# Scores on 64-row halves of the array, another order of zero writes, weight splits and gathers in a retention, mixture-of-experts and MLP kernel

## The chip, the cores and the metric

The kernel runs on one core of a Trainium2 chip. The metric is the device time of one execution in microseconds (us), the median over several runs. The core has a matrix engine (PE, with its weight loads shown as PEld), two elementwise engines (DVE and POOL), an activation engine (ACT), and SP, which here only issues transfers. POOL issues the indirect transfers (gathers). Sixteen DMA engines move the data.

## What is computed

```python
scores = scale * q @ k^T                                  # 4 batches, 8 heads, 576 tokens, 64 per head
Dmat = where(rel >= 0, gamma ** rel, 0)                   # rel = query position - key position
x = (scores * Dmat) @ v                                   # retention, -> 2304 tokens x 512
noisy = x @ w_gate + log1p(exp(x @ w_noise)) * noise      # 8 experts
top2, weights = two largest per token, softmax over them
for each expert e:                                        # 2304 x 512 -> 1024 -> 512
    out[its tokens] += weight * relu(x @ w1[e]) @ w2[e]
h = out @ w_in                                            # 512 -> 2048
result = (h * cos(h)) @ w_out                             # 2048 -> 512
```

## The kernel before, in words

Three stages follow one another on the matrix engine, and each prepares the next. Every float32 product is written as one instruction in the code and shows as two passes in the trace, so 8 products of a tile are 16 PE instructions.

**Tiles.** Retention runs over 20 tiles of 128 tokens, five per batch, the fifth with 64 rows from each of two halves ("tail"). One step `j` of the loop `for j in range(-2, NTILE + 1)` has the work of several tiles in it: `load_tile(j + 4)` issues the loads of Q (`qr`, L329), K (`kb`, L335) and K, V row-wise (`kv`, L343) on SP's queue, in order behind the stores of finished rows (`xs<-xr`, four per tile, L514) and, at the end of some steps, a 1 MB write of zeros into the unused part of the experts' output (`zero_overflow`, L373, `ys<-c_zero`). `decay(j + 2)` multiplies Q by its decay factors (L419 `qt<-qr`, on POOL from tile 4 on). `scores(j + 1)` makes K·Q for two heads at a time: a head has 64 dimensions, and two heads lie one above the other in the 128 rows. K is kept in a tile with zeros, rows 0 to 63 in one copy and rows 64 to 127 in another, so that each of the 8 products runs over all 128 rows (L445) and the zeros drop the other head. DVE multiplies each half of the result by the mask (L446, `am`). `outputs(j)` (L469, L474, L488) makes the attention rows; L474 has 64 result columns per product, in the left or right half of the array. `gate` and `gate_t` (L501, L521) start the choice of experts.

**Routing.** After the last tile of a group (6, 6, 4 and 4 tiles) a generator `routing(g)` counts where each token stands in its expert's list. It needs DVE for many small operations (`sa`, `sb`, L646 and L647, among them) and PE for counting ("rank", L606 to L615) and for tables (L638, `ptab<-sb,sa`). Its steps are let in by a planner: `spent(pe, dve)` adds the planned time of what was just written out, and `pump()` writes routing steps as long as the planned DVE queue is less than a slack ahead of PE. So the numbers given to `spent` decide how early routing stands on the engines.

**First expert.** The first layer of expert 0 for its first 320 tokens (`layer1(0, 0, True)`, L797) needs only the first groups; it starts at 123.96 us. It and its second layer (`layer2(0, 0, True)`, L818) are the loop `for k, _ in enumerate(post)`, with the rest of the routing pumped in between. In it stand the splits of expert 0's second weights `b0` to `b3` into a high and a low part (`split_unit`: ACT copies `hb`, L289; the engine named subtracts, `lb`, L290; then the next weight load is issued) at the steps `B_AT`, and more zero writes, at the steps `ZERO[i] - 20`. When the last group's table is there, `gidx` (L668) has the token numbers, POOL gathers three blocks of rows (L727, `rows<-xs,gidx`), PE turns them (L764), ACT and DVE split them, and `layer1(0, 1)` follows (L797, first at 167.00 us).

**Last layer.** After the eight experts, nine blocks of 256 tokens go through `fetch` (16 gathers on POOL, L1152, `y<-ys,slot`), `turn2` (weighted sum, turn, split into `x2h` and `x2l`), `mlp1` (PE L1192; then per part `g`, DVE and ACT make `t`, `gh`, and DVE or POOL makes `gl`, L1210) and `mlp2` (L1222). `fetch(0)` reads only the rows that are written early; `fetch(1)` and later read all rows of `ys`, so they stand behind the last expert's stores (L831, L835). Block 0 also has the splits of the last weights in it, `b0` to `b3` and `d0` to `d3`. `FS0` is the number of gathers of block 1 issued per step of `mlp1` in block 0, `SP0` the steps that have a split, `SPP` those on POOL, `GLP0` how many `gl` of block 0 go to POOL.

Of the kernel before, what the change touches and what calls it, by code (L numbers as in the profile page):

```python
# [10 lines left out]
F32 = mybir.dt.float32  # L11
# [6 lines left out]
OP = mybir.AluOpType  # L18
# [6 lines left out]
HP = H // 2  # L25
NC = 5
# [16 lines left out]
PHB = 3  # L43
STB = 3
QPOOL = 4
ZERO = (11, 13, 22, 27, 27, 29, 33)
LOOK = 4
WJ = 3
T0_AT = ()
GLP = 8  # L50
GLP0 = 4
FS = 1
FS0 = 1
SPP = (0, 3, 6, 9)
SP0 = (0, 1, 2, 3, 4, 5, 6, 7, 8, 9)

CG_1 = (6, 8, 9, 11, 13, 15)
CG_2 = (1, 2, 3, 4, 5)
# [18 lines left out]
B_US = 1.1  # L77
# [4 lines left out]
PE_LAT = 0.2  # L82
SPLIT_POOL = False
L1_WAIT = 2
B_AT = (0, 1, 2, 24)
B_POOL = range(99)
TURN_AT0 = (1, 1, 2, 3, 4)
GN = max(z - a for a, z in GRP)
EARLY_N = GRP[EARLY - 1][1] // NC * S + GRP[EARLY - 1][1] % NC * 128
# [125 lines left out]
def moe_kernel(ctx, tc, x, out, dbg=None, phases="ABC"):  # L215
    nc = tc.nc
# [14 lines left out]
    ps = ctx.enter_context(tc.tile_pool(name="ps", bufs=1, space=PSUM))  # L231
# [65 lines left out]
    ca = A.enter_context(tc.tile_pool(name="ca", bufs=1))  # L297
# [13 lines left out]
    bs = {n: cb[:, a:b] for n, (a, b) in OB.items()}  # L311
    dq0 = ca.tile([128, HP * 128 + (NC - 1) * HP], F32, name="dq0")
    dq = [dq0[:, :HP * 128]] + [ca.tile([128, HP * 128], F32, name=f"dq{c}") for c in range(1, NC)]
    KB = []
    for i in range(LOOK):
        t = ca.tile([128, HP, 2, 128], F32, name=f"kb{i}")
        eng = nc.gpsimd if i else nc.vector
        eng.memset(t[:64, :, 1, :], 0.0)
        eng.memset(t[64:, :, 0, :], 0.0)
        KB.append(t)  # L320
    KBT = ca.tile([128, HP, 2, TAIL], F32, name="kbt")
    SB = [ca.tile([128, HP, 128], F32, name=f"sb{i}") for i in range(2)]
# [2 lines left out]
    KT, KV, QR, QT, VT, AM, XT, XR, G = {}, {}, {}, {}, {}, {}, {}, {}, {}  # L325
# [4 lines left out]

    def load_k(j):
        b, c = divmod(j, NC)
        kb, src = (KB[(4 * b + c) % LOOK], x["kt"][4 * b + c]) if c < 4 else (KBT, x["ktt"][b])
        for s in range(2):
            nc.sync.dma_start(kb[s * 64:(s + 1) * 64, :, s, :],  # L335
                              src[s * 64:(s + 1) * 64].rearrange("p (a t) -> p a t", a=HP))
        KT[j] = kb

    def load_kv(j):
        b, c = divmod(j, NC)  # L340
# [44 lines left out]
    for i in range(2):  # L385
        t = rt.tile([128, GN, 2 * E], F32, name=f"lg{i}")
# [49 lines left out]
    def scores(j):  # L436
        b, c = divmod(j, NC)
        am = wk.tile([128, HP, 2, 128], F32, name="am", bufs=2)
        if c < 4:
            for h2 in range(2):  # L440
                p = ps.tile([128, 2, 2, 128], F32, name="ph", bufs=PHB)
                for i in range(2):
                    hp = 2 * h2 + i
                    for s in range(2):
                        nc.tensor.matmul(p[:, i, s, :], KT[j][:, hp, s, :], QT[j][:, hp, :], start=True, stop=True)  # L445
                nc.vector.tensor_tensor(  # L446
                    am[:, 2 * h2:2 * h2 + 2].rearrange("p a s q -> p (a s) q"),
                    p.rearrange("p a s q -> p (a s) q"),
                    bs["mask"][:, None, :].to_broadcast([128, 4, 128]), op=OP.mult)
                AM[j] = am  # L450
                yield
        else:
            p = ps.tile([128, HP, 128], F32, name="ph", bufs=PHB)
            for hp in range(HP):
                nc.tensor.matmul(p[:, hp, :], KT[j][:, hp].rearrange("p s q -> p (s q)"), QT[j][:, hp, :],
                                 start=True, stop=True)
            nc.vector.tensor_tensor(am[:, :, 0, :], p, bs["maskt"][:, None, :].to_broadcast([128, HP, 128]),
                                    op=OP.mult)
            AM[j] = am
            yield  # L460
# [383 lines left out]
    def spent(pe, dve=0.0):  # L844

        at["P"] += pe
        if dve:
            at["D"] = max(at["D"], at["P"] + PE_LAT) + dve
# [48 lines left out]
    for j in range(-2, NTILE + 1):  # L897
        if j >= 0:
            load_tile(j + LOOK)
        if j == WJ - 2:  # L900
            for _ in range(3):
                load_unit()
        if 0 <= j + 2 < NTILE:
            decay(j + 2)
        if j == -2:
            late = late_consts()
            next(late)
        pump()
        tail = j % NC == NC - 1
        if 0 <= j + 1 < NTILE:  # L910
            decay_v(j + 1)
            for _ in scores(j + 1):
                spent(0.87, 0.6)
                pump()
        if j >= -1:
            next(late, None)
        turn_early()
        if 0 <= j - 1 < NTILE:
            gate(j - 1)
            spent(0.37, 0.6)  # L920
        pump()
        fill(LF[0])
        if 0 <= j < NTILE:
            outputs(j)
            spent(1.75 if tail else 2.8)
        fill(LF[1])
        pump()
        turn_early()
        if 0 <= j - 1 < NTILE:
            gate_t(j - 1)  # L930
            spent(0.11, 0.13)
            for gi, (_, z) in enumerate(GRP):
                if z == j:
                    gens.append([routing(gi), 0])
        fill(LF[2])
        if j < NTILE:
            pump()
        for i in range(7):
            if ZERO[i] == j:
                zero_overflow(i)  # L940
        if j >= WJ and state["split"] < 4:
            split_unit(nc.gpsimd if SPLIT_POOL else nc.vector)
            if not SPLIT_POOL:
                spent(0, 1.1)
# [7 lines left out]
    for k, _ in enumerate(post):  # L952
        spent(0.33, L_US)
        pump()
        if k in T0_AT and not gens:
            turn(0, late[0])
            late[0] += 1
        if k in B_AT:
            split_unit(nc.gpsimd if k in B_POOL else nc.vector)
            if k not in B_POOL:  # L960
                spent(0, B_US)
        for i in range(7):
            if ZERO[i] == NTILE + k:
                zero_overflow(i)
# [211 lines left out]
    def mlp1(i, parts):  # L1176

        cw = state["d"]
        P, T = {}, {}

        def fl(t):
            return t.rearrange("p a b -> p (a b)")

        for s in range(10):
            if s < 8:
                w = W[8 * E + s]
                p = bank_h([128, 2, 256])
                for f in range(2):
                    k = 0
                    for a, b in PASSES:  # L1190
                        for dc in range(DC):
                            nc.tensor.matmul(p[:, f, :], w[a][:, dc, f * 128:(f + 1) * 128], X2[i][b][:, dc, :],  # L1192
                                             start=(k == 0), stop=(k == 3 * DC - 1))
                            k += 1
                P[s] = fl(p)
                t = T[s] = cw.tile([128, 512], F32, name="t", bufs=4)
                nc.scalar.activation(t, P[s], AF.Identity, scale=INV2PI, bias=cbias[:, 0:1])  # L1197
                nc.vector.tensor_scalar(t, t, -MAGIC, None, op0=OP.add)  # L1198
                nc.vector.scalar_tensor_tensor(t, t, -2 * PI, P[s], op0=OP.mult, op1=OP.add)
                nc.vector.tensor_scalar(t.bitcast(I32), t.bitcast(I32), 0x7FFFFFFF, None, op0=OP.bitwise_and)  # L1200
            if 0 <= s - 1 < 8:
                t = T[s - 1]
                nc.scalar.activation(t, t, AF.Sin, scale=-1.0, bias=cbias[:, 1:2])  # L1203
                nc.vector.tensor_tensor(t, t, P[s - 1], op=OP.mult)
            if 0 <= s - 2 < 8:
                g = s - 2
                gh = cw.tile([128, 2, 256], F32R, name=f"gh{g}")
                gl = cw.tile([128, 2, 256], F32R, name=f"gl{g}")
                nc.scalar.activation(fl(gh), T[g], AF.Copy)
                (nc.gpsimd if g < (GLP if i else GLP0) else nc.vector).tensor_tensor(  # L1210
                    fl(gl), T[g], fl(gh.bitcast(F32)), op=OP.subtract)
                parts.append((gh, gl))
            yield
# [21 lines left out]
    def drain(g):  # L1235
        for _ in g:
            pass

    def steps(g, n):
        for _ in range(n):  # L1240
            next(g, None)
# [12 lines left out]
    for e in range(E):  # L1254
# [3 lines left out]
        n = 0  # L1258
# [43 lines left out]
    for i in range(len(blocks)):  # L1302
        parts = []
        n = 0
        fg = fetch(i + 1)
        for _ in mlp1(i, parts):
            if n in SP0 and state["split"] < len(units):
                split_unit(nc.gpsimd if n in SPP else nc.vector)
            steps(fg, FS if i else FS0)
            n += 1  # L1310
        while state["split"] < len(units):
            split_unit()
        drain(fg)
        drain(turn2(i + 1))
        if i + 1 < len(blocks):
            mlp2(i, (0, 1), parts)
        else:
            mlp2(i, (0,), parts)
            mlp2(i, (1,), parts, ((0, DM // 2), (DM // 2, DM)))
# [18 lines left out]
```

## Time and profile before

| | |
|---|---|
| timed, 3 runs | 1069.2 us median (1066.33 to 1070.52) |
| the profiled execution, its own time | 1059.2 us |
| its span in the trace | 1057.3 us |
| PE busy | 995.3 us (94%) |
| PEld / DVE / POOL / ACT busy | 928.5 / 688.6 / 445.8 / 370.1 us |
| mean granted clock of PE | 0.966 |

The span runs from the first to the last instruction; the time of an execution has 1.9 us more around it. The timed runs lie above the profiled one by 7 to 11 us. A busy time is a sum over stages with different limits. "Idle before, releaser" in a row tells how long the engine stood still ahead of an instruction and what came last.

### The profile page before, as it was taken

The numbers are of one execution on the slowest core, as the hardware profiler recorded it, in microseconds if no ns is written. First come the engines' busy times: TensorE is split into PE (matmuls) and PEld (weight loads), VectorE is DVE, ScalarE is ACT, GpSimd is POOL, SyncE is SP. The second block draws the span as 40 slices with busy tenths as digits, with TensorE's granted clock in tenths as the row PEclk, the third lists the DMA queues.
The fourth block names the chain that finished last, engine by engine and source line by source line (L and its number), as shares of the span: only waits on it lengthen the run. The fifth ranks groups of instructions, "written<-read, shape, count | busy, mean of one in ns | idle before, by whom it ended". The sixth has DMA issues, their size and how long they took to land.

```text
span 1057.3 us, 17808 instructions
## 1 busy us (share of the span) xinstructions
PE 995.3 (94%) x6845; PEld 928.5 (88%) x6845; DVE 688.6 (65%) x1364; ACT 370.1 (35%) x657; POOL 445.8 (42%) x439
## 2 busy tenths in 40 slices
PE   8989986879899999999899989999999999999998
PEld 7778875869898989989899989798988989899897
DVE  4688971638587676858586447865848567484662
ACT  2422410323141323323142334543535445353451
POOL 6343436351506142341500064736547474564711
PEclk9999988869999999999999999989999999999999
DMA  9898494336576565657563544211010110101110
GB/s 277 270 261 266 120 295 121 100 101 182 157 209 185 180 204 164 215 147 238 160 209 102 141 138 135 73 33 48 21 46 23 43 35 32 50 18 46 30 24 20
DMA packets 85846, 135.37 MB, mean 128 GB/s; under 512 B 13376, under 2 KB 51648, under 8 KB 85760
## 3 DMA queue, kind: packets, MB, share of 16 engines
q1 hardware_dynamic: 76048, 113.74, 36.2%
q0 software_dynamic: 9568, 20.20, 7.3%
q8 instruction: 55, 0.90, 0.4%
q10 hardware_dynamic: 144, 0.27, 0.1%
q14 instruction: 31, 0.25, 0.1%
HBM read 106.25 MB, written 35.26 MB: 134 GB/s over the span
## 4 chain that ended last, share of the span: by engine, by line
PE 84%; DMA 5%; issue 4%; DVE 4%; SPq 1%; ACT 1%; POOL 0%; ACTq 0%; DVEq 0%; POOLq 0%
PE py L1222 18%; PE ph L818 14%; PE ph L797 10%; PE ph L1192 9%; PE pt L797 8%; PE pt L1192 5%; DMA qr<-qt 4%; PE ptab L797 4%; PE ptab L818 3%; PE pt L818 3%; PE ptab L1192 3%; PE ph L445 1%; PE py L818 1%; PE py L469 1%; PE py L474 1%
## 5 line engine op out<-in xcount | busy, mean ns | idle before, releaser
L722 POOL DMA_INDIRECT rows<-xs,gidx x140 | 139.1, 993 | 227.9 <-DVE xt L755 186.7
L1152 POOL DMA_INDIRECT y<-ys,slot x144 | 139.9, 972 | 56.3 <-issue 26.5
L1210 POOL TENSOR_TENSOR gl<-t,gh 128x512 fp32r<-128x512 f32 x68 | 88.6, 1303 | 140.8 <-issue 111.1
L818 PE MATMUL ph<-hh,hb 128*128 128x360 f32 (+2 forms) x312 | 98.8, 317 | 4.9 <-issue 4.6
L818 PE MATMUL ph<-hh,lb 128*128 128x360 f32 (+2 forms) x312 | 98.9, 317 | 4.2 <-issue 4.1
L818 PE MATMUL ph<-hl,hb 128*128 128x360 f32 (+2 forms) x312 | 98.9, 317 | 2.5 <-issue 2.5
L1200 DVE TENSOR_SCALAR t<-t 128x512 int32<-128x512 int32 x72 | 72.8, 1011 | 2.5
L1171 DVE SCALAR_TENSOR_TENSOR y<-y,wts,y 128x128 f32<-128x128 f32 x72 | 34.4, 510 | 59.1 <-DMA y<-ys,slot 52.1
L1198 DVE TENSOR_SCALAR t<-t 128x512 f32<-128x512 f32 x72 | 37.4, 519 | 51.0 <-ACT t L1197 51.0
L747 ACT ACTIVATE xh<-xt 128x512 fp32r<-128x512 f32 (+1 forms) x35 | 21.6, 617 | 137.7 <-DVE xt L755 118.7
L818 PEld LDWEIGHTS ph<-hh,lb 128*128 128x128 f32 x312 | 60.9, 195 | 6.8 <-issue 6.7
L818 PEld LDWEIGHTS ph<-hh,hb 128*128 128x128 f32 x312 | 61.4, 197 | 5.1 <-issue 5.1
L818 PEld LDWEIGHTS ph<-hl,hb 128*128 128x128 f32 x312 | 60.8, 195 | 4.3 <-issue 4.3
L1203 ACT ACTIVATE t<-t,cbias 128x512 f32<-128x512 f32 x72 | 51.9, 722 | 32.9 <-DVE t L1200 32.1
L802 ACT ACTIVATE hh<-pt 128x256 fp32r<-128x256 f32 (+2 forms) x48 | 20.0, 416 | 110.0 <-PE pt L797 77.2
L1222 PE MATMUL py<-hd,gl 128*128 128x512 f32 (+1 forms) x152 | 57.7, 380 | 0.8 <-DVE gl L1210 0.8
L1222 PE MATMUL py<-hb,gl 128*128 128x512 f32 (+1 forms) x152 | 58.4, 384 | 0.0
L1222 PE MATMUL py<-lb,gh 128*128 128x512 f32 (+1 forms) x152 | 58.4, 384 | 0.0
L1222 PE MATMUL py<-hb,gh 128*128 128x512 f32 (+1 forms) x152 | 58.3, 384 | 0.0
L290 POOL TENSOR_TENSOR lb<-st,hb 128x1024 fp32r<-128x1024 f32 x7 | 16.9, 2423 | 97.4 <-PE ptab L797 58.1
L797 PE MATMUL ph<-xh,ha 128*128 128x360 f32 (+3 forms) x236 | 47.7, 321 | 10.5 <-issue 6.1
L797 PE MATMUL ph<-xl,ha 128*128 128x360 f32 (+3 forms) x236 | 49.0, 322 | 9.2 <-issue 9.0
(307 smaller groups left out, 2747.2 us busy)
## 6 DMA issues: line engine op xcount, KB each, us to landing
st<-w SPq DMA_DIRECT2D x64, 512.0 KB
kv<-kv SPq DMA_DIRECT2D x16, 512.0 KB
ci<-wi SPq DMA_DIRECT2D x16, 512.0 KB
wc<-cy SPq DMA_DIRECT2D x32, 256.0 KB
ci<-wo SPq DMA_DIRECT2D x16, 512.0 KB
st<-wc SPq DMA_DIRECT2D x16, 512.0 KB
ys<-c_zero SPq DMA_DIRECT2D x7, 1024.0 KB
qr<-qt SPq DMA_DIRECT2D x20, 256.0 KB
```

What stands on the lines that cost most here:

```text
L722: nc.gpsimd.indirect_dma_start(out=t[:, g, :], out_offset=None, in_=xs.rearrange("n (a d) -> (n a) d", a=4), in_offset=bass.IndirectOffset ...
L747: nc.scalar.activation(hi, src, AF.Copy)
L797: nc.tensor.matmul(p[:, :n], w[a][:, dc, (f % 2) * 128:(f % 2 + 1) * 128], XE[e, g][b][:, dc, :n], start=(i == 0), stop=(i == 3 * DC - 1))
L818: nc.tensor.matmul(p[:, :n], w[a][:, f % 2, c * 128:(c + 1) * 128], HE[e, g][b][:, f, :n], start=(i == 0), stop=(i == 3 * FC - 1))
L1152: nc.gpsimd.indirect_dma_start(out=t[:, g, :], out_offset=None, in_=(ys if i else ys[:FIRST]).rearrange("n (a d) -> (n a) d", a=4), in_off ...
L1171: nc.vector.scalar_tensor_tensor(y0[:, g], y1[:, g], w1, y0[:, g], op0=OP.mult, op1=OP.add)
L1192: nc.tensor.matmul(p[:, f, :], w[a][:, dc, f * 128:(f + 1) * 128], X2[i][b][:, dc, :], start=(k == 0), stop=(k == 3 * DC - 1))
L1198: nc.vector.tensor_scalar(t, t, -MAGIC, None, op0=OP.add)
L1200: nc.vector.tensor_scalar(t.bitcast(I32), t.bitcast(I32), 0x7FFFFFFF, None, op0=OP.bitwise_and)
L1203: nc.scalar.activation(t, t, AF.Sin, scale=-1.0, bias=cbias[:, 1:2])
L1210: (nc.gpsimd if g < (GLP if i else GLP0) else nc.vector).tensor_tensor(fl(gl), T[g], fl(gh.bitcast(F32)), op=OP.subtract)
L1222: nc.tensor.matmul(ps_[tb][:, :c1 - c0], parts[f // 2][b][:, f % 2, tb * 128:(tb + 1) * 128], w[a][:, f % 2, c0:c1], start=(f + k == 0), s ...
```

## The change

The scores no longer multiply zeros: each product uses the 64 rows of one head, and the results of the upper and of the lower rows go to two PSUM tiles. K is loaded by one transfer of 2 KB rows instead of two of 512-byte pieces, and the clears of the padded K tiles are gone (2 on DVE, 6 on POOL). Two of the zero writes leave the tile loop. The splits of expert 0's second weights move from POOL to DVE and to later steps. In block 0 of the last layer the gathers of block 1 go first on POOL, and splits and `gl` change engines.

```diff
-ZERO = (11, 13, 22, 27, 27, 29, 33)
+ZERO = (22, 27, 27, 29, 33, 38, 44)
-FS0 = 1
-SPP = (0, 3, 6, 9)
-SP0 = (0, 1, 2, 3, 4, 5, 6, 7, 8, 9)
+FS0 = 4
+SP0 = (0, 1, 3, 5, 7, 9)
-B_AT = (0, 1, 2, 24)
-B_POOL = range(99)
+B_AT = (0, 5, 10, 24)
...
         if c < 4:
-            for h2 in range(2):
-                p = ps.tile([128, 2, 2, 128], F32, name="ph", bufs=PHB)
-                for i in range(2):
-                    hp = 2 * h2 + i
-                    for s in range(2):
-                        nc.tensor.matmul(p[:, i, s, :], KT[j][:, hp, s, :], QT[j][:, hp, :], start=True, stop=True)
-                nc.vector.tensor_tensor(
-                    am[:, 2 * h2:2 * h2 + 2].rearrange("p a s q -> p (a s) q"),
-                    p.rearrange("p a s q -> p (a s) q"),
-                    bs["mask"][:, None, :].to_broadcast([128, 4, 128]), op=OP.mult)
+            pp = [ps.tile([128, HP, 128], F32, name="ph", bufs=PHB) for _ in range(2)]
+            for hp in range(HP):
+                for s in range(2):
+                    h = slice(s * 64, s * 64 + 64)
+                    nc.tensor.matmul(pp[s][:, hp, :], KT[j][h, hp, :], QT[j][h, hp, :], start=True, stop=True)
+            for s in range(2):
+                nc.vector.tensor_tensor(am[:, :, s, :], pp[s], bs["mask"][:, None, :].to_broadcast([128, HP, 128]),
+                                        op=OP.mult)
...
-                spent(0.87, 0.6)
+                spent(0.87 if (j + 1) % NC == NC - 1 else 0.5, 0.6)
...
-            split_unit(nc.gpsimd if k in B_POOL else nc.vector)
-            if k not in B_POOL:
-                spent(0, B_US)
+            split_unit()
+            spent(0, B_US)
...
-                (nc.gpsimd if g < (GLP if i else GLP0) else nc.vector).tensor_tensor(
+                (nc.gpsimd if i or g > 4 else nc.vector).tensor_tensor(
...
             if n in SP0 and state["split"] < len(units):
-                split_unit(nc.gpsimd if n in SPP else nc.vector)
+                split_unit()
             steps(fg, FS if i else FS0)
             n += 1
+        drain(fg)
+        tg = turn2(i + 1)
         while state["split"] < len(units):
-            split_unit()
-        drain(fg)
-        drain(turn2(i + 1))
+            split_unit(nc.gpsimd)
+            steps(tg, 1)
+        drain(tg)
```

Line numbers of the changed kernel are smaller by 4 to 6 than those named above. The planner, fed with the smaller 0.5, also moves routing. On PE, at the end of expert 0's first 320 tokens, the last table stood between second-layer products before (20 more of them in groups of three followed, 60 instructions, before the turns):

```order
L638 LDWEIGHTS sa
L638 MATMUL ptab<-sb,sa 128x144
L531 MATMUL ph<-gf,spread 128x40 x4
L686 LDWEIGHTS ones
L686 MATMUL ph<-run,ones 128x8
L687 LDWEIGHTS ones
L687 MATMUL ph<-adj,ones 128x8
L818 MATMUL py_2033<-hh_1678,hb_1791 128x320
```

The same place in the changed kernel, where L813 is L818, L633 is L638 and L759 is L764:

```order
L633 LDWEIGHTS sa
L633 MATMUL ptab<-sb,sa 128x144
L526 MATMUL ph<-gf,spread 128x40 x4
L681 LDWEIGHTS ones
L681 MATMUL ph<-run,ones 128x8
L682 LDWEIGHTS ones
L682 MATMUL ph<-adj,ones 128x8
L759 MATMUL pt<-ident,rows 128x128 x8
L759 MATMUL ph<-ident,rows 128x128 x4
```

The table, and with it the token numbers for the gather, now comes after the last second-layer product, directly ahead of the turns of the gathered rows.

On DVE, the splits of expert 0's second weights now stand between the routing's operations and the first layer's `hl`, in the changed kernel:

```order
L641 TENSOR_SCALAR sa<-it_163,vf 128x128
L642 TENSOR_SCALAR sb<-it_163,vf,cs 128x144
L286 TENSOR_TENSOR lb_1704<-st,hb_1703 128x1024
L798 SCALAR_TENSOR_TENSOR hl_1651<-ph,hh_1650 128x320 x2
L286 TENSOR_TENSOR lb_1731<-st,hb_1730 128x1024
L798 SCALAR_TENSOR_TENSOR hl_1651<-ph,hh_1650 128x320
L641 TENSOR_SCALAR sa<-it_163,vf 128x128
```

Before, all four stood on POOL, between the last tile's V and the gather of rows, where now no split is left.

On POOL, in block 0 of the last layer, before (`y_7115` and `y_7284` and the eight after them are block 1's rows):

```order
L290 TENSOR_TENSOR lb_7110<-st,hb_7109 128x1024
L1152 DMA y_7115<-ys,slot_83 128x128 x2
L1210 TENSOR_TENSOR gl_7189<-t,gh_7188 128x512
L1152 DMA y_7115<-ys,slot_83 128x128
L1210 TENSOR_TENSOR gl_7232<-t,gh_7231 128x512
L290 TENSOR_TENSOR lb_7236<-st,hb_7235 128x1024
L1152 DMA y_7115<-ys,slot_83 128x128
L1210 TENSOR_TENSOR gl_7275<-t,gh_7274 128x512
L1152 DMA y_7284<-ys,slot_83 128x128
L1210 TENSOR_TENSOR gl_7319<-t,gh_7318 128x512
L1152 DMA y_7284<-ys,slot_83 128x128
L290 TENSOR_TENSOR ld_7364<-st,hd_7363 128x1024
```

and in the changed kernel, from the last gather tile of block 0 on:

```order
L1146 DMA y_6740<-ys,slot_83 128x128 x4
L1146 DMA y_7091<-ys,slot_83 128x128 x4
L1146 DMA y_7134<-ys,slot_83 128x128 x4
L1146 DMA y_7175<-ys,slot_83 128x128 x4
L1146 DMA y_7222<-ys,slot_83 128x128 x4
L1204 TENSOR_TENSOR gl_7374<-t,gh_7373 128x512
L1204 TENSOR_TENSOR gl_7386<-t,gh_7385 128x512
L1204 TENSOR_TENSOR gl_7390<-t,gh_7389 128x512
L286 TENSOR_TENSOR ld_7398<-st,hd_7397 128x1024
L286 TENSOR_TENSOR ld_7415<-st,hd_7414 128x1024
```

The sixteen gathers of block 1 now stand in one run, ahead of all of POOL's other work in that block.

## Rows read from the trace of the kernel before

**Rows 1.** The page's head: span, and busy time of each engine.

```profile
span 1057.3 us, 17808 instructions
PE 995.3 (94%) x6845; PEld 928.5 (88%) x6845; DVE 688.6 (65%) x1364; ACT 370.1 (35%) x657; POOL 445.8 (42%) x439
```

**Rows 2.** Windows: stretch and length, engines' busy time, granted clock, DMA share, GB/s.

```profile
0.00:100.00 100.00, 89.44 (x857) 76.11 (x858) 68.99 (x202) 29.54 (x65) 47.40 (x67) 0.98 0.92 266
696.00:1057.00 361.00, 357.87 (x2322) 326.91 (x2320) 224.08 (x340) 158.60 (x278) 188.42 (x174) 1.00 0.12 33
```

**Rows 3.** Groups of instructions, 0 to 125 us, PE and PEld.

```profile
L445 PE MATMUL ph<-qt,kb 128*128 128x128 f32 x256 | 35.6, 295 | 8.7 <-POOL qt L419 6.0 <-DVE qt L419 1.9 <-DMA kb<-kt 0.6
L474 PE MATMUL py<-am,vt 128*64 128x128 f32 x256 | 17.5, 279 | 0.0
...
L445 PEld LDWEIGHTS ph<-qt,kb 128*128 128x128 f32 x256 | 33.1, 208 | 11.1 <-POOL qt L419 7.1 <-DVE qt L419 2.4 <-DMA kb<-kt 1.0
L474 PEld LDWEIGHTS py<-am,vt 128*64 128x64 f32 x256 | 13.6, 136 | 2.3 <-issue 0.6 <-POOL vt L427 0.2
```

**Rows 4.** Waits, 0 to 125 us: total, times, longest.

```profile
POOL qt L419 <- DMA qr<-qt: 32.0, 8, 7.4
...
DVE am L446 <- PE ph L445: 1.9, 5, 0.7
```

**Rows 5.** Timeline of SP's queue and of POOL, late tiles: start, duration.

```profile
97.62 0.59 SPq L373 DMA_DIRECT2D ys<-c_zero  x1
98.31 0.57 SPq L329 DMA_DIRECT2D qr<-qt  x1
...
106.84 1.26 POOL L419 TENSOR_TENSOR qt<-qr,dq 128x512 f32<-128x512 f32 x1 [7.42 <-DMA qr<-qt]
```

**Rows 6.** Timeline of POOL, DVE and PE, first expert's first layer.

```profile
128.49 7.04 POOL L290 TENSOR_TENSOR lb<-st,hb 128x1024 fp32r<-128x1024 f32 x3 [9.84 <-PE ph L797]
...
127.81 0.25 DVE L646 TENSOR_SCALAR sa<-it,vf 128x128 f16<-128x128 f16 x1
...
130.87 2.41 DVE L646 TENSOR_SCALAR sa<-it,vf 128x128 f16<-128x128 f16 x1
...
136.43 1.44 PE L797 MATMUL ph<-xh,ha 128*128 128x320 f32 x4 [4.27 <-DVE hl L803]
...
142.68 0.75 PE L797 MATMUL ph<-xl,ha 128*128 128x320 f32 x4
```

**Rows 7.** Timeline of PE and POOL, last table to the turns.

```profile
153.44 0.53 PE L638 MATMUL ptab<-sb,sa 128*128 128x144 f16 x4
155.45 0.39 PE L818 MATMUL py<-hh,hb 128*128 128x320 f32 x1
164.34 1.03 PE L764 MATMUL pt<-ident,rows 128*128 128x128 f32 x8
...
157.14 0.95 POOL L727 DMA_INDIRECT rows<-xs,gidx  x1 [0.30 <-issue]
```

**Rows 8.** Timeline of DVE, ACT, POOL and PE, block 0 of the last layer.

```profile
652.25 1.21 DVE L290 TENSOR_TENSOR lb<-st,hb 128x1024 fp32r<-128x1024 f32 x1
...
645.73 0.69 ACT L1197 ACTIVATE t<-pt,cbias 128x512 f32<-128x512 f32 x1 [7.86 <-DMA ys<-y]
...
684.91 0.94 POOL L1152 DMA_INDIRECT y<-ys,slot  x1 [0.30 <-issue]
...
687.59 0.35 DVE L1171 SCALAR_TENSOR_TENSOR y<-y,wts,y 128x128 f32<-128x128 f32 x1 [0.89 <-DMA y<-ys,slot]
...
689.40 1.01 PE L1192 MATMUL ptab<-x2h,hc 128*128 128x256 f32 x3 [3.95 <-issue]
```

**Rows 9.** Windows behind block 0, and behind a run of 16 gathers; columns as in group 2.

```profile
688.70:695.50 6.80, 6.09 (x28) 6.10 (x29) 0.69 (x1) 2.29 (x4) 0.00 (x0) 0.50 0.25 89
...
624.00:632.00 8.00, 4.50 (x22) 3.58 (x21) 2.62 (x8) 0.91 (x2) 3.96 (x5) 0.92 0.16 42
```

**Rows 10.** That run, grouped: POOL, 607 to 630 us.

```profile
L1152 POOL DMA_INDIRECT y<-ys,slot x16 | 16.8, 1048 | 26.8 <-DMA ys<-y 22.3 <-issue 4.6
```

More of the change, by code (lines that the diff above doesn't have):

```diff
@@ L49 @@
 T0_AT = ()
-GLP = 8
-GLP0 = 4
 FS = 1
-FS0 = 1
-SPP = (0, 3, 6, 9)
-SP0 = (0, 1, 2, 3, 4, 5, 6, 7, 8, 9)
+FS0 = 4
+SP0 = (0, 1, 3, 5, 7, 9)
 CG_1 = (6, 8, 9, 11, 13, 15)
@@ L315, in moe_kernel @@
     for i in range(LOOK):
[L316 to L319, printed above, removed]
+        t = ca.tile([128, HP, 128], F32, name=f"kb{i}")
         KB.append(t)
@@ L332, in load_k @@
         b, c = divmod(j, NC)
-        kb, src = (KB[(4 * b + c) % LOOK], x["kt"][4 * b + c]) if c < 4 else (KBT, x["ktt"][b])
+        if c < 4:
+            KT[j] = KB[(4 * b + c) % LOOK]
+            nc.sync.dma_start(KT[j].rearrange("p a t -> p (a t)"), x["kt"][4 * b + c])
+            return
         for s in range(2):
-            nc.sync.dma_start(kb[s * 64:(s + 1) * 64, :, s, :],
-                              src[s * 64:(s + 1) * 64].rearrange("p (a t) -> p a t", a=HP))
-        KT[j] = kb
+            nc.sync.dma_start(KBT[s * 64:(s + 1) * 64, :, s, :],
+                              x["ktt"][b][s * 64:(s + 1) * 64].rearrange("p (a t) -> p a t", a=HP))
+        KT[j] = KBT
     def load_kv(j):
```

## The prediction, made before the changed kernel was run

> **What bounds the kernel now.** I read the page's head first. PE is busy for 995.3 of 1057.3 us [rows 1], so a change helps only by giving PE less to do, by ending one of its waits, or by bringing its clock back. The windows then say where that is to be had. From 696 us on PE works 357.87 of 361.00 us at a granted clock of 1.00 [rows 2]; nothing in the diff touches the products there, so I count no gain behind 696. In the first 100 us PE is busy 89.44, and the DMA engines 0.92 of the time at 266 GB/s [rows 2]: the reader should see two resources near their limits at once, so that relief of one alone uncovers the other. The groups by line show what PE waits for there: 8.7 us ahead of the scores, mostly for the decayed Q [rows 3], and the waits show that POOL itself, which makes it, waited 32.0 us for Q's transfer [rows 4]. So the tile stage hangs on its loads first, on PE second. The timelines of the first expert and of the last layer's block 0 give the other two places where PE stands still.
>
> **Scores and loads in the tile loop.** Eight products stay eight products, so by count nothing is saved. What may be saved is that the two halves of the array work side by side. No product of this kernel used row halves, so the price has two ends. The upper bound of the time is the 35.6 us that the scores have now. The lower one is the nearest other use of half an array, L474, which puts its results in column halves: the same 256 passes of 128 columns take 17.5 us [rows 3]. The saving is so 0 to 18.1 us, 0 to 1.1 us per tile. The end nearer to the new products is L474, since they too come in pairs on different halves, but with one difference: their weight loads keep 128 columns, where L474 loads 64, and loads of the scores are busy for 33.1 us against 13.6 [rows 3]. I take two thirds, 12 us of PE work.
>
> The Trainium skill, "TensorEngine Tiling (Array Packing)", Key Properties, says that such tiles load weights and multiply in parallel, which would give about the L474 end, but also that a change of the tiling mode drains the engine. "TensorE: Matmul & The Clock Gate", LDWEIGHTS, says that a load's time goes by its columns and not its rows, which speaks against the change: by it alone the pairs would stay near 35.6 us. By the first page the sum would be the forecast below or a few us better, by the second it would be rival (a). No row here has a row half, so the trace decides neither.
>
> PE's saving alone does not bring the end of the stage forward where PE waits for loads. There the zero writes count. Two of 1 MB each (1.05 million bytes) leave the loop; at 266 GB/s [rows 2] each is 3.9 us of all engines, together 7.9. They stand directly ahead of Q: the one issued at 97.62 is followed by Q at 98.31, which POOL gets at 106.84 after a wait of 7.42 [rows 5]. K's new long pieces carry the same bytes; I take nothing for them, and the clears that go (8, at the start, beside the first loads) nothing either. Behind that last wait PE has no more long gap to the stage's end, so there the work itself counts: one tile's saving, 1.1. Sum: 7.9 + 1.1 = 9 us. Bounds: if the zero writes only hurt the Q behind them, and the products gain nothing, about 3; if all waits ahead of the scores go (8.7) and four tiles' savings count (4.4), 13.
>
> The two mask products now run after all eight products instead of one after the first half. DVE waited only 1.9 us for scores in the whole stage [rows 4], so it is mostly behind PE anyway, and a mask used in the next step of the loop has a tile's time to be made: nothing, covered by the outputs, L469 to L488. If that cover fails, the price is in the rivals.
>
> **First expert.** Three splits on POOL take 7.04 us from 128.49 on, and in that time DVE's `sa` takes 2.41 us where it took 0.25 before [rows 6]. `hl` stands behind it, so PE waits 4.27 us and then runs at half speed (four products in 1.44 us where 0.75 is usual) from 136.43 to 142.68 [rows 6], which costs half of 6.25, 3.1. With the splits on DVE, spread out, both go: 7.4 us. The four splits cost DVE 1.21 each [rows 8], 4.8 us; DVE has room, since by the order they stand beside operations of 0.25, and one split delays an `hl` by 1.2 us at most while PE has other products. I take nothing.
>
> Against that stands what the order shows: the last table now comes after the last second-layer product. Before, from 155.45 to 164.34 PE had 8.9 us of these products [rows 7] while rows were gathered and landed. Now PE has nothing in that time. From the table (ending at 153.97) to the third gather's end (157.14 + 0.95 = 158.09) it is 4.1 us [rows 7], and a gather's data are used 1.74 us after its end (684.91 + 0.94 to 687.59) [rows 8], so 5.9 us from the table to the turns. Of these, 1.5 lay on PE's path before as well (153.97 to 155.45). New wait: 4.4 us. PE's clock fell after the wait of 4.27, so it may fall here too, up to 3.1; I take half, 1.5. Net of the place: 7.4 - 4.4 - 1.5 = 1.5 us gained. Bounds: +3 without the clock's fall, and -4 if seven zero writes and the weight loads on the same queues hold the gathered rows up by 5.5 us more (1.4 zero writes of 3.9).
>
> **Block 0 of the last layer.** Now PE waits 3.95 us for block 1's rows [rows 8] because the gathers of block 1 wait their turn on POOL behind splits and `gl`; then it runs for 6.8 us at a granted clock of 0.50, its lower level, 1.2 GHz [rows 9]. PE was busy 6.09 of that, half of which is lost, 3.0. With the gathers first, the last of them ends not before: the last expert's stores land at about 645.7 (ACT waits for them till then) [rows 8], and 16 gathers at 1.25 each (16.8 us busy and 0.30 between them [rows 10]) end at 666. Then POOL has three `gl` and two splits, and block 1's rows are there well before 685, when block 0's products end. 3.95 + 3.0 = 7 us gained. But a run of 16 gathers has a price of its own: in the run of 607 to 629 [rows 10], PE was idle for 3.5 of the 8 us from 624 on [rows 9], with nothing that it waited for but issue. The new run of 16 should do the same: 7 - 3.5 = 3.5. Bounds: +7 without that stall, -5 if it is more than three times as long.
>
> **Sum.** 9 + 1.5 + 3.5 = 14 us off the profiled execution's own time, 1059.2, to 1045. The timed runs have a median 10 us above it, 1069.2, and nothing in the rows says that the difference goes away, so 1069.2 - 14 = **1055**.
>
> **Rivals.**
> (a) The row halves give nothing, for the weight loads run one after another, or the loads stay the bound: the tile stage gives 3 instead of 9. For it: weight loads busy 33.1 of the 35.6 us. Against: the passes of L474. 1069.2 - 3 - 1.5 - 3.5 = 1061.
> (b) The exposed gather of the first expert takes more than it gives: place at -4. For it: the cover of 8.9 us is gone, and zero writes come before the gather. Against: only two zero writes more than before stand in this stretch, 7.9 us of transfers in some 40. 1069.2 - 9 + 4 - 3.5 = 1061; with the clock lower for longer, 1064.
> (c) The change doesn't do what it says: the tile stage runs by stores, V and K, and PE's saved time becomes waits, while the two places behind give and take the same: 1066 to 1070.
> (d) Slower. The scores now hold two of the three `ph` tiles until DVE has masked them, each after all eight products; routing and the first layer use `ph` too. If DVE is late, PE waits in every tile. It decides from where the wait is over 14/16 = 0.9 us per tile in 16 tiles; at 1.6 us, the result is 1069.2 - 14 + 26 = 1081, and at 1.2 us 1074. For it: DVE is 0.69 busy in these 100 us [rows 2] and more late. Against: the tile where `ph` is needed next comes a gate and an output later.
>
> **How the numbers follow.** The forecast, 1049 to 1060, has 0.45; (a) 0.20, (b) 0.12, (c) 0.12, (d) 0.11. The range of 8 in 10 leaves out (d) and the gains that take all upper bounds at once (13 + 3 + 7 = 23, 1046): 1044 to 1068. A change under 0.5% (5.3 us) is about what a measurement of this kernel can't tell from none. Faster than 1063.9 are the forecast, (a) with most of its weight and two thirds of (b): 0.45 + 0.18 + 0.09 = 0.72. Same: the rest of (a) and (b), 0.05, and most of (c), 0.09, together 0.14. Slower: (d) and 0.03 of (c), for 1069.2 is itself known only to within a few us, 0.14.
>
> **What would show it.** Right: pairs of score passes that start together, as those of L474 do; the first expert's first layer starts near 115 instead of 123.96; no `sa` over 2 us in it; a wait of about 6 us ahead of the turns of gathered rows; gaps by issue in PE near 657 to 668, and no wait for `x2h` at the end of block 0. Wrong: scores that still take 35 us in all, waits for `ph` tiles on PE, a POOL gather that is done and a turn that starts 5 us later, or a block 0 that has its old length because the issue gaps ate what the earlier gathers gave.

## The result

The changed kernel took 1056.57 us (median of 4 runs, 1053.68 to 1058.88), the kernel before 1067.76 beside it (4 runs, 1065.31 to 1070.52): a ratio of 0.9882, with a 95% interval of 0.9851 to 0.9913. That is 11 us faster, against 14 predicted, and within the range. Repeated, it gave 0.9901 (0.9866 to 0.9935).

The two profiled executions do not show this: the span is 1057.0 us after and was 1057.3 before. The head of the page after the change, to be read beside [rows 1]:

```profile
span 1057.0 us, 17774 instructions
PE 990.5 (94%) x6845; PEld 918.6 (87%) x6845; DVE 681.5 (64%) x1368; ACT 370.4 (35%) x657; POOL 431.1 (41%) x427
```

The profile of before was 6 us faster than any run of that kernel timed beside it, and that of after was the slowest of its runs. So I compare stages and not spans. The starts of stages, in us, read from the timeline of PE in the two profiles:

| start of | before | after | lead |
|---|---|---|---|
| first expert's first layer, first part | 123.7 | 112.8 | 10.9 |
| its second layer | 147.2 | 127.9 | 19.3 |
| second part of the first layer | 167.0 | 154.6 | 12.4 |
| first layer of expert 1 | 210.9 | 200.0 | 10.9 |
| block 0 of the last layer | 638.9 | 636.6 | 2.3 |
| second products of block 1 | 715.2 | 714.9 | 0.3 |

The tile stage gave its 10.9 us, the first expert's two places added 1.5, and that was lost again before expert 1. Then 8.6 us were lost between 200 and 637, where no line differs. The windows of that part show what differs, first before, then after, then the changed kernel once more (`e1_again`); columns as in [rows 2]:

```profile
210.90:638.90 428.00, 405.69 (x2698) 395.49 (x2697) 284.80 (x524) 128.56 (x216) 132.74 (x131) 0.96 0.58 170
```

```profile
200.00:636.60 436.60, 408.94 (x2699) 398.03 (x2698) 284.76 (x523) 128.39 (x216) 131.40 (x132) 0.95 0.58 167
```

```profile
199.70:639.50 439.80, 411.54 (x2698) 399.92 (x2698) 285.14 (x523) 128.91 (x216) 131.03 (x131) 0.94 0.56 166
```

The same products at a lower clock, and some more idle time. Over all twelve experiments this part took 424.8 to 440.8 us. The experiments were run in three groups of four; the runs of before beside them had medians of 1070.6, 1058.4 and 1067.4 us, and in the second group this part took 424.8 to 431.0 in every kernel. So part of its length goes with the group. Whether the change adds to it is not shown; a cost of 8.6 us in every run would use up most of the tile stage's lead, and yet 11 us were timed.

### The profile page after: what moved, and what is told of

Its sections match the earlier page's. It is cut to its first block, busy times and chain, and to the rows that moved or that the text cites. A ratio compares the mean times of both kernels' runs of the same rounds, so it can differ in the third digit from the quotient of the medians.

```text
span 1057.0 us, 17774 instructions
## 1 busy us (share of the span) xinstructions
PE 990.5 (94%) x6845; PEld 918.6 (87%) x6845; DVE 681.5 (64%) x1368; ACT 370.4 (35%) x657; POOL 431.1 (41%) x427
## 4 chain that ended last, share of the span: by engine, by line
PE 88%; issue 5%; DVE 4%; DMA 2%; SPq 1%; ACT 1%; POOL 0%; DVEq 0%; POOLq 0%; ACTq 0%
PE py L1216 19%; PE ph L813 14%; PE ph L792 10%; PE ph L1186 10%; PE pt L792 8%; PE pt L1186 7%; PE ptab L792 4%; PE ptab L813 3%; PE ptab L1186 3%; PE pt L813 3%; PE py L813 1%; PE py L483 1%; PE py L469 1%; PE ph L441 1%; PE py L464 1%
## 5 line engine op out<-in xcount | busy, mean ns | idle before, releaser
L813 PE MATMUL ph<-hl,hb 128*128 128x360 f32 (+2 forms) x312 | 100.2, 321 | 4.7 <-issue 4.5
L813 PE MATMUL ph<-hh,lb 128*128 128x360 f32 (+2 forms) x312 | 100.1, 321 | 3.1 <-issue 3.0
L813 PE MATMUL ph<-hh,hb 128*128 128x360 f32 (+2 forms) x312 | 100.0, 321 | 2.7 <-issue 2.7
L1165 DVE SCALAR_TENSOR_TENSOR y<-y,wts,y 128x128 f32<-128x128 f32 x72 | 38.3, 568 | 56.2 <-DMA y<-ys,slot 48.7
L1192 DVE TENSOR_SCALAR t<-t 128x512 f32<-128x512 f32 x72 | 35.0, 487 | 56.2 <-ACT t L1191 56.2
L1194 DVE TENSOR_SCALAR t<-t 128x512 int32<-128x512 int32 x72 | 67.3, 934 | 2.5
L813 PEld LDWEIGHTS ph<-hh,hb 128*128 128x128 f32 x312 | 62.3, 200 | 5.6 <-issue 5.6
L813 PEld LDWEIGHTS ph<-hh,lb 128*128 128x128 f32 x312 | 61.9, 198 | 6.1 <-issue 6.1
L813 PEld LDWEIGHTS ph<-hl,hb 128*128 128x128 f32 x312 | 61.6, 197 | 5.4 <-issue 5.4
L1216 PE MATMUL py<-ld,gh 128*128 128x512 f32 (+1 forms) x152 | 57.5, 378 | 0.0
L1216 PE MATMUL py<-hd,gh 128*128 128x512 f32 (+1 forms) x152 | 57.5, 378 | 0.0
L797 ACT ACTIVATE hh<-pt 128x256 fp32r<-128x256 f32 (+2 forms) x48 | 20.0, 417 | 101.2 <-PE pt L792 81.7
L286 DVE TENSOR_TENSOR la<-st,ha 128x1024 fp32r<-128x1024 f32 x36 | 44.7, 1241 | 12.6 <-ACT ha L285 12.4
```

Of the source, the lines that this page charges most:

```text
L286: lo_engine.tensor_tensor(lo.rearrange("p a b -> p (a b)"), st, hi.bitcast(F32).rearrange("p a b -> p (a b)"), op=OP.subtract)
L813: nc.tensor.matmul(p[:, :n], w[a][:, f % 2, c * 128:(c + 1) * 128], HE[e, g][b][:, f, :n], start=(i == 0), stop=(i == 3 * FC - 1))
L1165: nc.vector.scalar_tensor_tensor(y0[:, g], y1[:, g], w1, y0[:, g], op0=OP.mult, op1=OP.add)
L1216: nc.tensor.matmul(ps_[tb][:, :c1 - c0], parts[f // 2][b][:, f % 2, tb * 128:(tb + 1) * 128], w[a][:, f % 2, c0:c1], start=(f + k == 0), s ...
```

## The profile after, place by place

**Tile stage.** Groups of PE and PEld from 0 to 125 us, then the wait of POOL for Q, beside [rows 3, 4]:

```profile
L441 PE MATMUL ph<-qt,kb 64*128 64x128 f32 x256 | 21.3, 296 | 4.9 <-DVE sb L642 2.6 <-DVE qt L415 1.1 <-DVE am L443 0.8
...
L441 PEld LDWEIGHTS ph<-qt,kb 64*128 64x128 f32 x256 | 17.5, 196 | 8.9 <-POOL qt L415 3.5 <-DVE qt L415 2.4 <-DVE am L443 1.2
```

```profile
POOL qt L415 <- DMA qr<-qt: 24.7, 10, 4.2
```

The scores fell from 35.6 to 21.3 us, and PE's wait for the decayed Q on POOL (6.0 us) is gone from their row; their weight loads still wait 3.5 us for it, 7.1 before. POOL's wait for Q fell from 32.0 to 24.7 us. All 16 passes of a tile show as one row, here in the changed kernel:

```profile
26.21 1.16 PE L441 MATMUL ph<-qt,kb 64*128 64x128 f32 x16
```

**First expert.** Timeline of PE and POOL around the gather, to be read beside [rows 6, 7]:

```profile
112.84 0.71 PE L792 MATMUL ph<-xh,ha 128*128 128x320 f32 x3 [0.16 <-ACT xh L742]
...
143.40 0.53 PE L633 MATMUL ptab<-sb,sa 128*128 128x144 f16 x4
...
150.72 2.00 PE L759 MATMUL pt<-ident,rows 128*128 128x128 f32 x8 [5.13 <-DMA rows<-xs,gidx]
...
154.57 1.35 PE L792 MATMUL pt<-xh,ha 128*128 128x296 f32 x4 [0.61 <-ACT xh L742]
...
145.05 0.99 POOL L722 DMA_INDIRECT rows<-xs,gidx  x1 [34.93 <-DMA st<-w]
```

The wait of 4.27 us is gone. In its place stands one of 5.13 us, for the gathered rows, and behind it four products take 1.35 us where the same four take 0.78 in `e7_bpool`: the lower clock, as after the old wait.

**Block 0.** Timeline of POOL and PE, then two windows of 8 us:

```profile
644.03 0.95 POOL L1146 DMA_INDIRECT y<-ys,slot  x1 [19.18 <-DMA ys<-y]
...
665.00 0.95 POOL L1146 DMA_INDIRECT y<-ys,slot  x1 [0.30 <-issue]
...
661.72 0.41 PE L1186 MATMUL pt<-x2l,xh 128*128 128x256 f32 x2 [0.83 <-issue]
```

```profile
660.00:668.00 8.00, 4.34 (x16) 3.43 (x17) 3.87 (x6) 3.23 (x5) 4.73 (x5) 0.78 0.39 115
668.00:676.00 8.00, 8.00 (x30) 6.37 (x29) 6.70 (x11) 6.11 (x11) 2.89 (x3) 0.80 0.10 17
```

The 16 gathers start when the last stores land, and from 656 on PE halts again and again with nothing but issue to wait for: 3.7 us lie idle in 660 to 668 (8 - 4.34). The first products of block 0 took 31.7 us (636.6 to 668.3) instead of 23.0: 4.6 us of the 8.7 more are idle, the rest is that the same products took longer. The old wait ahead of block 1 is gone: block 0's second products took 23.6 us instead of 27.5, block 1's first ones 23.0 instead of 25.8.

## The experiments

"Start" is the first product of the first expert (L797 or its line in the variant), 123.7 us before (123.71 in the timeline, where the text ahead of the prediction has 123.96), 112.8 after. It comes from one profile per run: the two of the kernel before are 2.3 us apart, the five with the changed tile stage 1.5. Ratios are to the kernel before in the same group.

**The changed kernel and the kernel before once more.** Nothing edited.

> The changed kernel once more, for a second profile and a tighter interval: the first profile of it was its slowest run, that of the kernel before its fastest. Expected 1054 to 1059 us, ratio 0.985 to 0.992. If block 0 of the last layer loses by the run of 16 gathers in itself, its first layer takes about 31 us here too (23.0 before); if that was chance, about 23 to 26 us.

> The kernel before once more, for a second profile: the first one is 6 us below every timed run of it. From the first layer of expert 1 to the first product of the last layer it took 428.0 us there, and 437 to 441 us in all profiles of the changed kernel and its variants, though no line of that part differs. Theory E, that profile was a chance draw: 436 to 441 us here too, about 1069 us. Theory F, the change costs that part 9 us: 428 us again.

The changed kernel: 0.9901, start 112.3, first products of block 0 30.9 us: that stall is no chance. In other kernels with the same gathers these products took 23.6 to 31.7 us, so the size of the stall varies (see block 0 below). The kernel before: start 121.4, middle part 424.9 us. E is not met by its numbers, for this group was quicker as a whole, and F (the change costs that part 9 us) is not borne out: beside it the variants of the changed kernel took 424.8, 427.7 and 430.9 us there. A smaller cost is not ruled out. This copy of the kernel before had a ratio of 0.9957 (0.9931 to 0.9983) to itself. So ratios half a per cent apart are not told apart by times; the stages have to do it.

**Full rows again.**

```diff
-                    nc.tensor.matmul(pp[s][:, hp, :], KT[j][h, hp, :], QT[j][h, hp, :], start=True, stop=True)
+                        nc.tensor.matmul(p[:, i, s, :], KT[j][:, hp, s, :], QT[j][:, hp, :], start=True, stop=True)
...
+        t = ca.tile([128, HP, 2, 128], F32, name=f"kb{i}")
```

> The changed kernel with the scores over all 128 rows again, K padded and loaded in two transfers as before; all else as changed. Theory A, the tile stage gained by PE time of the scores (35.6 to 21.3 us): 9 us or more come back, about 1066 us, and the first expert starts at about 122 us. Theory B, as predicted, it gained by the zero writes that left: it starts at about 115 us, 1058 to 1059 us.

1067.68 us, 0.9972 (0.9948 to 0.9995), start 119.8. By the time most of the gain is lost; by the start 7 of the 10.9 us, between A's 122 and B's 115 and nearer to A. But the edit undoes two things, the products and K's layout with its loads, which the next runs take apart.

**Half rows from the padded K**, loaded and cleared as before:

```diff
-                    nc.tensor.matmul(pp[s][:, hp, :], KT[j][h, hp, :], QT[j][h, hp, :], start=True, stop=True)
+                    nc.tensor.matmul(pp[s][:, hp, :], KT[j][h, hp, s, :], QT[j][h, hp, :], start=True, stop=True)
```

> The changed kernel with half-row scores, but K padded, cleared and loaded in two transfers of 512-byte pieces as before. Theory A1, the tile stage gained by PE time: the first expert starts at 112 to 114 us, 1058 to 1061 us. Theory A2, it gained by K's long pieces and the clears that went, not by PE: it starts at about 119 us as with full rows, 1067 us.

Start 121.8, and 0.9914. The scores were quick, as the group from 0 to 125 us shows, but PE waited:

```profile
L441 PE MATMUL ph<-qt,kb 64*128 64x128 f32 x256 | 23.4, 305 | 12.9 <-POOL qt L415 7.1 <-DVE qt L415 2.1 <-DMA kb<-kt 2.1
```

By the start A1 fell, and A2 holds: with the old loads, 10 us less work on PE (33.6 us for full rows in `e2_fullrow`, 23.4 here) came out as waits, and the stage was no shorter than with full rows. POOL waited 40.5 us for Q, against 24.7 in the changed kernel. The time does not follow: A2 had 1067 us, and 0.9914 is nearly the ratio of the changed kernel. The unedited copy of the kernel before, at 0.9957 in this group, covers about half of that; the rest is open. The next two take the new load apart: without the eight clears, and with two transfers of long pieces.

```diff
-        eng.memset(t[:64, :, 1, :], 0.0)
-        eng.memset(t[64:, :, 0, :], 0.0)
```

> Half-row scores, K still in the padded layout and loaded in two transfers of 512-byte pieces, but without the eight clears (nothing reads the padding). With the clears the first expert started at 121.8 us, in the changed kernel at 112.3 to 113.8. Theory G, the clears at the start cost it: start at 113 to 117 us, first gate of a tile at 13 to 14 us instead of 17. Theory H, the short pieces or the two transfers do: start at 118 to 122 us.

```diff
-            nc.sync.dma_start(KT[j].rearrange("p a t -> p (a t)"), x["kt"][4 * b + c])
+            for s in range(2):
+                r = slice(s * 64, s * 64 + 64)
+                nc.sync.dma_start(KT[j][r].rearrange("p a t -> p (a t)"), x["kt"][4 * b + c][r])
```

> The changed kernel with K loaded in two transfers of 64 rows each, in long pieces of 2 KB. Theory H1, the length of the pieces is what counts: the first expert starts at 112 to 115 us as in the changed kernel. Theory H2, the number of transfers on SP's queue counts: 117 to 121 us. The time follows, 1 us per us.

Start 120.4 without the clears (0.9984), 116.5 with two long transfers (0.9967), and 112.3 to 113.8 with one, in the four profiles that have the changed tile stage (`e1_again`, `e4_finalold`, `e7_bpool`, `e8_fs1`) and the first. So G fell, and H1 and H2 share it: 121.8 to 120.4 for the clears, which is within the spread of the profiles, 3.9 us for the long pieces, 3.7 us for one transfer instead of two. These are differences of single profiles, and the changed kernel itself was not timed in this group; the ratio of the two long transfers, 0.9967, has lost more than their start. That a transfer costs something by itself shows on SP's queue, first in the changed kernel, then with two long transfers:

```profile
68.97 0.38 SPq L328 DMA_DIRECT2D kb<-kt  x1
```

```profile
66.47 1.11 SPq L330 DMA_DIRECT2D kb<-kt  x2
```

**The same products, neighbours on the same half.**

```diff
-            for hp in range(HP):
-                for s in range(2):
+            for s in range(2):
+                for hp in range(HP):
```

> The changed kernel with the same eight score products in another order: first the four on the upper rows, then the four on the lower ones, so that neighbours use the same half. Loads and everything else as changed. If pairs on different halves run side by side and that is what shortens the scores, the scores take about 30 to 36 us in all instead of 21. Theory I, this PE time counts once the loads are quick: the first expert starts 6 us later or more, about 119 us. Theory J, the stage hangs on loads and other waits and the PE time is nearly all given back as waits: 0 to 3 us later, 112 to 116 us.

Two rows of this kernel, the group from 0 to 125 us and one tile's passes in the timeline:

```profile
L441 PE MATMUL ph<-qt,kb 64*128 64x128 f32 x256 | 29.1, 295 | 1.8 <-DVE qt L415 1.6 <-DVE am L443 0.3
```

```profile
19.98 1.71 PE L441 MATMUL ph<-qt,kb 64*128 64x128 f32 x16
```

1.71 us per tile instead of 1.16: it is the neighbour on the other half that makes the pair quick. Start 115.6, ratio 0.9946 (0.9925 to 0.9967). PE's 7.8 us came out as 2.8 us at the stage's end, which is J at its upper end, and not I.

**The zero writes back in the tile loop.**

```diff
-ZERO = (22, 27, 27, 29, 33, 38, 44)
+ZERO = (11, 13, 22, 27, 27, 29, 33)
```

> The changed kernel with two zero writes back in the tile loop, as before. Theory A: about 2 us lost at the start of the first expert, 1057 to 1059 us. Theory B, the zero writes' 7.9 us: the first expert starts at about 120 us, 1064 us, less what the first expert's gather gets back with two zero writes fewer in its stretch, 1 to 2 us.

0.9901 (0.9865 to 0.9937), and the start was 109.38 us: 3 us earlier than without them, against both theories. First the changed kernel, then this one, windows of 80 to 90 us:

```profile
80.00:90.00 10.00, 6.85 (x73) 5.45 (x68) 9.60 (x47) 1.15 (x3) 3.55 (x3) 0.88 0.69 209
```

```profile
80.00:90.00 10.00, 8.32 (x92) 6.96 (x92) 9.90 (x31) 2.50 (x6) 4.55 (x4) 0.83 0.89 282
```

In the changed kernel the DMA engines have room here (0.69, and 0.89 with the writes). PE stands still for 2.8 us, since DVE is late with a routing mask (L594), and in this variant it does not. `e12_best`, with the same writes, started at 110.7. Why the writes let DVE come to the mask earlier is not shown, nor what they cost with K's old loads, for they were put back only beside the new one.

**Splits of the first expert back on POOL.**

```diff
-B_AT = (0, 5, 10, 24)
+B_AT = (0, 1, 2, 24)
...
-            split_unit()
+            split_unit(nc.gpsimd)
```

> The changed kernel with the four splits of expert 0's second weights on POOL again, at their old steps. Theory as predicted: the stall of DVE's operations and the half clock come back, the first layer of the first expert takes 23 us instead of 15, and about 7 us are lost, 1065 to 1067 us. Rival: the last table waits for routing on DVE anyway and the gather behind it is the end of the chain, so only 2 to 3 us are lost, 1060 to 1062 us.

0.9887 (0.9868 to 0.9905): nothing lost. PE and POOL in the timeline:

```profile
112.76 0.71 PE L792 MATMUL ph<-xh,ha 128*128 128x320 f32 x3 [0.16 <-ACT xh L742]
...
122.95 1.44 PE L792 MATMUL ph<-xh,ha 128*128 128x320 f32 x4 [4.09 <-DVE hl L798]
...
144.19 0.53 PE L633 MATMUL ptab<-sb,sa 128*128 128x144 f16 x4
...
152.00 1.04 PE L759 MATMUL pt<-ident,rows 128*128 128x128 f32 x8
...
154.54 0.78 PE L792 MATMUL pt<-xh,ha 128*128 128x296 f32 x4 [1.07 <-DVE xl L743]
...
145.33 0.99 POOL L722 DMA_INDIRECT rows<-xs,gidx  x1 [10.51 <-DMA st<-w]
```

The wait of 4.09 us and the half clock are back, and yet the second part starts at 154.54, as in the changed kernel (154.57), and the gather at 145.33 (145.05). PE's products fill the time up to the gathered rows now: the edit, which also takes the splits out of the planner's account of DVE, moved the last table, so that second-layer products stand behind it again (146.20 to 152.00), as before the change. It is thus a trade of the stall against the uncovered gather, not the stall by itself, and the two come out level. The rival's time holds, and more fully than written: nothing at all is lost. Its reason, that the table waits for routing on DVE, is not what the traces show: DVE's last `sb` ends at 141.93 here and at 142.52 in the changed kernel, and the table's last products, at 144.19 and 143.40, stand directly behind second-layer products on PE.

**Block 0 as before, and with the gathers one per step.**

```diff
-FS0 = 4
-SP0 = (0, 1, 3, 5, 7, 9)
+GLP0 = 4
+FS0 = 1
+SPP = (0, 3, 6, 9)
+SP0 = (0, 1, 2, 3, 4, 5, 6, 7, 8, 9)
```

> The changed kernel with block 0 of the last layer as before (gathers one per step, splits and gl on the engines of before). Theory C, the new run of 16 gathers costs more by its stall and the clock behind it than the wait that it removes: 1 to 3 us faster than the changed kernel, 1053 to 1056 us. Theory D, as predicted, the new order is worth 3.5 us: 1060 us.

```diff
-FS0 = 4
+FS0 = 1
```

> The changed kernel with the gathers of block 1 again one per step of the first products (7 in a run, then between gl). If the run of 16 is what stalls block 0: its first layer takes 24 to 26 us instead of 31, no gaps by issue; block 1's rows come later, so a wait of 2 to 5 us at its start may return; in all 1 to 4 us faster than the changed kernel. If the length of the run is not the cause, the gaps stay and it is the same or slower.

With the old block 0: 0.9895 (0.9868 to 0.9922); from block 0 to the second products of block 1 it took 75.6 us, against 78.3 and 77.7 in the two profiles of the changed kernel. Theory C holds by the stage; the time is no different. With one gather per step (0.9927) the first products took 23.0 us again, and no gap by issue was left. All profiles with the run of 16 have such gaps in block 0's first products or right behind them, and none with 7 gathers or the old order has, so the run of 16 is the cause. How much it costs varies. In `e7_bpool`, in the same group as the one gather per step, the gaps came so late that the first products took 23.6 us, and 2.9 us lay idle in the window behind them:

```profile
627.70:651.30 23.60, 23.41 (x194) 23.09 (x192) 17.08 (x29) 12.62 (x19) 12.83 (x12) 1.00 0.55 150
651.30:659.00 7.70, 4.81 (x13) 2.58 (x14) 6.13 (x10) 2.89 (x5) 4.46 (x5) 0.87 0.38 118
```

From block 0 to the second products of block 1 that kernel took 74.3 us, less than any other profile; the kernel before took 76.3 and 74.8. So the new order loses 2 to 3 us in the changed kernel's two profiles and nothing there; what sets when the gaps begin is not shown. With one gather per step the stage took 79.7 us, for the gathers that are left over stand ahead of the splits on POOL, and PE waited for a split:

```profile
660.53 1.33 POOL L1204 TENSOR_TENSOR gl<-t,gh 128x512 fp32r<-128x512 f32 x1 [12.78 <-ACT gh L1203]
...
676.92 4.66 POOL L286 TENSOR_TENSOR ld<-st,hd 128x1024 fp32r<-128x1024 f32 x2
...
679.32 0.79 PE L1216 MATMUL py<-ld,gh 128*128 128x512 f32 x1 [7.64 <-POOL ld L286]
```

**Both of the edits that helped their stage**, the zero writes and block 0 of before, in one kernel.

> The changed kernel with the two zero writes back in the tile loop and block 0 of the last layer as before, since both gained in their own stage: the first expert's second part started 4 us earlier with the former, and block 0 with block 1 took 2 to 3 us less with the latter. Expected 4 to 6 us faster than the changed kernel, ratio to before 0.983 to 0.986. Rival: the middle part gives it back by its clock, 0.988 to 0.991.

1053.93 us, 0.9879 (0.9844 to 0.9913), start 110.7, block 0 to block 1's second products 75.7 us. The stages keep what they had gained, and the time lies with the rival: against 0.9882 and 0.9901 it is not shown to be faster than the changed kernel.

## Why the prediction was right, and where it was not

**The tile stage** had 9 us and gave 10.9, but not by the terms written. The zero writes, 7.9 of the 9, gave nothing beside the new load: leaving them in was 2 to 3 us better. K's new load, "I take nothing", gave 9.0 of it (clears 1.4, long pieces 3.9, one transfer fewer 3.7). The error was to price a load by its bytes. That the stage hung on how quickly SP's queue came to the next Q is argued from POOL's wait for it (24.7 us, and 40.5 with the old loads); this wait alone does not set the start, for `e3_zeroold` has 33.1 us of it and starts earlier. [rows 3] has only a hint of it: 0.6 of the 8.7 us ahead of the scores were K's own transfer. One at a time, the load (9.0), the pairs (2.8) and the zero writes (-3) make 9 of the 10.9. But such terms need not add up: the pairs, worth 2.8 beside the new load, were worth nothing beside the old one. The planner's smaller number was not tried alone.

**The scores.** 12 us less PE work were forecast, 14.3 measured (35.6 to 21.3), nearer to the end of L474. About three of them reached the stage's end (`e11_sameside`: 7.8 us of PE, 2.8 us of start), where the sum had 1.1. The Trainium skill, "TensorEngine Tiling (Array Packing)", Key Properties, has tiles load and multiply in parallel. The trace agrees: 1.16 us against 1.71 for the same products in the other order. The Trainium skill, "TensorE: Matmul & The Clock Gate", LDWEIGHTS, has a load's time go by its columns and not its rows. For a single load the trace agrees: 196 ns on average against 208, with 128 columns in each as before. But loads on the two halves overlap, and the time with a load of the scores under way fell from 33.1 to 17.5 us, so to read that rule against the change was wrong.

**The first expert.** Forecast 7.4 gained and 4.4 to 5.9 given back, net 1.5. Measured: from 112.8 to 154.6 41.8 us, from 123.7 to 167.0 43.3 before: net 1.5. The first layer took 15.1 us instead of 23.5 (8.4), and the rest 26.7 instead of 19.8 (6.9). Each term was a little small and the net was right. That was luck: `e7_bpool`, with the splits on POOL, took 41.8 us as well. Taking them off POOL moved the wait to behind the table and gained nothing, and where the 1.5 us come from is not shown.

**Block 0** had the wrong sign in the changed kernel: +3.5 forecast, about 2 lost. The wait that went was sized well: 7 us forecast, 6.7 measured (3.9 and 2.8). The price of the run of 16 was not: 3.5 forecast, from the idle time of one window, 8.7 measured, of which 4.6 are idle. The rest is that products took longer, in part at the lower clock (0.78 and 0.80 in the two windows from 660 on), where I had counted the lower clock only as something that goes away. In `e7_bpool` the stall was smaller and block 0 lost nothing.

**The sum.** By stages 10.9 + 1.5, less about 2 in block 0, and 1.5 in the rest of the first expert, is 9 us, if the middle part costs nothing; the timed difference is 11, with an interval of 9 to 16 us (0.9913 to 0.9851 of 1068). The forecast was right in the total partly by luck: one large term was right for another reason, and a wrong small one fell inside the range. Rival (a) had the row halves fail and lost, and (b) did not come, for the first expert gained 1.5. The time of (c) did not come, but its mechanism, PE's saved time becoming waits, is what `e6_halfpad` shows with the old loads. (d) did not come: the scores waited 0.8 us in all for `am`.

## What to carry to other kernels

Here a load in a queue that is nearly full cost by the number of its transfers (3.7 us) and the length of its pieces (3.9 us), not by its bytes alone: read what stands behind it in the queue. Products on the upper and lower 64 rows were quick only as neighbours on different halves (1.16 us against 1.71), and even then their saving showed only when the loads kept up. When a stall is taken away, look for the chain that ends last at the next meeting point: here it was the gather behind the last table, and PE's gain became a wait for it.

## What the hardware showed beyond that

A run of 16 indirect gathers stalled not only PE. ACT stood still twice in the same stretch with no releaser that the profile names in the core, in the changed kernel's timeline:

```profile
660.28 0.69 ACT L1191 ACTIVATE t<-ph,cbias 128x512 f32<-128x512 f32 x1 [4.08 <-remote]
...
667.53 0.69 ACT L1191 ACTIVATE t<-pt,cbias 128x512 f32<-128x512 f32 x1 [4.49 <-remote]
```

The second ends 1.6 us after the last gather (665.00 + 0.95), and with 7 gathers in a run (`e8_fs1`) neither engine showed such a halt. In `e1_again` ACT halted for 2.70 and 5.96 us at these two places, and there the profile names PE's products as what ended both. What PE waits for is not shown, nor whether ACT's halts in the changed kernel's first profile are its own.
